# A Fourier transform over 3008 rows, split as 47 x 64 instead of 94 x 32, with both of its small-matrix stages in tiles of the TensorE array

## The chip, the cores and the metric

The kernel runs on one core of a Trainium2 chip. The metric is the device time of one execution in microseconds (us), as a median of several executions. A trace (one profiled execution) gives every instruction's start and length on each engine. PE is TensorE's matrix multiply and PEld its weight load, DVE is VectorE, ACT ScalarE, POOL GpSimd, SP the sync engine; a q after a name (DVEq, SPq) is that engine's sequencer, which issues its instructions and transfers; "L207" is line 207 of the kernel that is being shown.

## The reference

```python
def _attn_ref(x):                       # x: 8 batches x 3008 x 256, float32
    X = np.fft.fft(x, axis=1)           # over s, 3008 long
    X = np.fft.fft(X, axis=2)           # over d, 256 long
    return X.real.astype(np.float32)

def _moe_ref(x, w_in, w_out):           # x: 24064 x 256, w_in 256 x 2048, w_out 2048 x 256
    h = x @ w_in
    g = h * (1.0 / (1.0 + np.exp(-1.702 * h)))
    return (g @ w_out).astype(np.float32)
```

## The kernel before

The transform over d is folded into the first weight matrix once. The transform over s is done in two stages: s = 32 a + j, with a = 0..93 and j = 0..31. A first stage multiplies, for each j, by a matrix over a; a second stage multiplies by a small matrix over j. Between them the data changes its layout by a trip through memory. Both stages of the next batch are cut into pieces which are strung between the large products of the present one (`hidden`, which writes the banks pa and pb, and `product`, which writes po; 384 steps in all).

```python
NA, NB = 94, 32

def mix1(b, c):                                   # first stage, two values of j; 8 such groups a batch
    ...
    ps = bank("ps1")
    for i in range(2):
        jj, o = 2 * c + i, i * D
        if jj:
            nc.tensor.matmul(ps[0:96, o:o + D], lhsT=mat(w1, jj), rhs=t[:, NB - jj, :], start=True, stop=True)
            continue
        ...                                       # j = 0: four products of half the width
    nc.scalar.copy(full[:, 2 * c:2 * c + 2, :].rearrange("p j d -> p (j d)"), ps[0:96, :])

def stage2(b, blk, cs):                           # second stage, half a block; 3 blocks a batch
    ...
    ps = bank("ps2")
    for g in range(4):
        nc.tensor.matmul(ps[:, g * 128:(g + 1) * 128], lhsT=t4[:, 4 * blk + g, cs * H:(cs + 1) * H],
                         rhs=m2[:, cs, :], start=True, stop=True)
    nc.scalar.copy(pq[:, cs, :], ps[:])
```

The banks of PSUM come from a ring of four (`bank`), shared with the two banks of `hidden`. The first batch has its own code: VectorE folds four pieces, the products follow, and the layout changes by a direct move from SBUF to SBUF (`shuffle_first`).

## Time and profile before

| | before |
|---|---|
| time, median of 3 (lowest, highest) | 1971.92 us (1971.71, 1972.20) |
| span of the profiled execution | 1969.6 us |
| TensorE / VectorE / ScalarE busy | 98% / 79% / 35% |
| first large product starts at | 54.6 us |
| the two stages' share of the chain that ended last | 2.3% + 2.3% |

The way to read it: TensorE is busy without a gap from 330 to 1800 us, so it alone sets the end there; only its time is worth saving. The lines for this stand in the prediction.

### The profile page before, as it was taken

How to read it: one execution, taken by the hardware profiler on the slowest of the kernel's cores; microseconds unless marked ns; L12 is line 12 of the kernel's file. 1: busy time of each engine (PE TensorE's matmuls, PEld its weight loads, DVE VectorE, ACT ScalarE, POOL GpSimd, SP SyncE). 2: the span in 40 equal slices, each digit the busy share in tenths (PEclk: the TensorE clock that was granted, in tenths of full speed). 3: DMA queues.
4: the chain of work that ended last, by engine and by line, in shares of the span. 5: the costliest groups of instructions: out<-in, count | busy, mean ns of one | idle time of the engine just before them, and what ended most of it. 6: DMA issues, size and time to landing. Idle time of an engine off the chain costs nothing.

```text
span 1969.6 us, 26665 instructions
## 1 busy us (share of the span) xinstructions
PE 1938.4 (98%) x9290; PEld 1724.3 (88%) x9290; DVE 1555.3 (79%) x2893; ACT 695.8 (35%) x970; POOL 793.8 (40%) x1065
## 2 busy tenths in 40 slices
PE   6999999999999999999999999999999999999997
PEld 4698899988989889888899888998899988989886
DVE  4778788888788777887788878887878888778776
ACT  2633333333333333333333333333333333333332
POOL 5476323543245332463325622255323543223232
PEclk8999999999999999999999999999999999999999
DMA  6720441216202252123422252221611213202201
GB/s 197 204 46 11 82 85 15 46 43 121 17 11 48 52 111 17 16 51 57 98 20 45 37 98 42 24 47 43 113 22 14 17 44 58 17 11 23 21 11 22
DMA packets 241837, 101.31 MB, mean 51 GB/s; under 512 B 209651, under 2 KB 232561, under 8 KB 239713
## 3 DMA queue, kind: packets, MB, share of 16 engines
q1 hardware_dynamic: 238965, 97.42, 28.7%
q10 hardware_dynamic: 2736, 2.18, 0.4%
q8 instruction: 73, 1.20, 0.3%
q14 instruction: 63, 0.52, 0.1%
HBM read 56.28 MB, written 45.76 MB: 52 GB/s over the span
## 4 chain that ended last, share of the span: by engine, by line
PE 96%; ACT 1%; DMA 1%; DVE 1%; issue 0%; POOL 0%; DVEq 0%; SPq 0%; POOLq 0%
PE po L464 58%; PE pa L397 16%; PE pb L397 16%; PE ps L189 2%; PE ps L277 2%; DMA raw<-in_moe_w_in_dram 0%; DMA t<-xt 0%; PE ps L241 0%; PE psw L366 0%; PE ps L240 0%; ACT g L314 0%; ACT r L322 0%; ACT r L321 0%; PE psa L372 0%; PE ps L192 0%
## 5 line engine op out<-in xcount | busy, mean ns | idle before, releaser
L438 POOL TENSOR_TENSOR s<-h 128x256 f32<-128x256 f32 (+2 forms) x376 | 273.8, 728 | 1098.2 <-ACT h L426 1026.6
L464 PE MATMUL po<-s,wt 128*128 128x256 f32 (+2 forms) x2256 | 600.0, 375 | 0.0
L401 ACT COPY v<-pa 128x512 f32<-128x512 f32 (+2 forms) x384 | 221.6, 577 | 893.1 <-PE pa L397 893.1
L411 DVE TENSOR_TENSOR h<-v,pb 128x512 f32<-128x512 f32 (+2 forms) x384 | 259.3, 675 | 336.6 <-PE pb L397 329.1
L464 PEld LDWEIGHTS po<-s,wt 128*128 128x128 f32 x2256 | 428.8, 190 | 48.3
L464 PE MATMUL po<-h,wo 128*128 128x256 f32 (+2 forms) x1632 | 469.9, 375 | 0.0
L421 DVE TENSOR_TENSOR h<-v,dif 128x512 f32<-128x512 f32 (+3 forms) x512 | 436.1, 871 | 13.2
L426 ACT ACTIVATE h<-h 128x1024 f32<-128x1024 f32 (+2 forms) x384 | 400.8, 1044 | 11.1 <-DVE h L421 11.1
L397 PE MATMUL pa<-pq,wcs 128*128 128x256 f32 (+2 forms) x1536 | 389.0, 376 | 0.0
L397 PE MATMUL pb<-pq,wcs 128*128 128x256 f32 (+2 forms) x1536 | 387.7, 375 | 0.0
L464 PEld LDWEIGHTS po<-h,wo 128*128 128x128 f32 x1632 | 310.1, 190 | 35.4
L414 DVE SCALAR_TENSOR_TENSOR dif<-nb,af,pb 128x256 f32<-128x256 f32 (+2 forms) x768 | 328.3, 469 | 0.0
L397 PEld LDWEIGHTS pb<-pq,wcs 128*128 128x128 f32 x1536 | 291.9, 190 | 33.0
L397 PEld LDWEIGHTS pa<-pq,wcs 128*128 128x128 f32 x1536 | 287.3, 190 | 33.0 <-issue 0.8
L439 POOL TENSOR_TENSOR s<-h 128x256 f32<-128x256 f32 (+2 forms) x376 | 277.6, 738 | 0.0
L442 DVE TENSOR_TENSOR s<-h,s 128x256 f32<-128x256 f32 (+2 forms) x376 | 211.3, 562 | 13.0
L464 PE MATMUL po<-h,wt 128*128 128x256 f32 (+2 forms) x752 | 220.5, 375 | 0.0
L464 PE MATMUL po<-s,wo 128*128 128x256 f32 (+2 forms) x752 | 220.5, 375 | 0.0
L441 DVE TENSOR_TENSOR s<-s,h 128x256 f32<-128x256 f32 (+2 forms) x376 | 175.3, 466 | 1.2 <-POOL s L438 1.2
L464 PEld LDWEIGHTS po<-s,wo 128*128 128x128 f32 x752 | 142.9, 190 | 16.1
L464 PEld LDWEIGHTS po<-h,wt 128*128 128x128 f32 x752 | 142.9, 190 | 16.1
L195 ACT COPY xt<-ps 96x512 f32<-96x512 f32 x56 | 32.5, 581 | 161.0 <-PE ps L189 151.2
(76 smaller groups left out, 878.0 us busy)
## 6 DMA issues: line engine op xcount, KB each, us to landing
out_dram<-os SPq DMA_DIRECT2D x512, 32.0 KB
Td<-xt SPq DMA_DIRECT2D x7, 1536.0 KB
t<-Td SPq DMA_DIRECT2D x7, 1536.0 KB
Xr<-in_x_dram SPq DMA_DIRECT2D x7, 1410.0 KB
xt<-in_x_dram SPq DMA_DIRECT2D x7, 1280.0 KB
xt<-Xr SPq DMA_DIRECT2D x7, 1200.0 KB
out_dram<-os SPq DMA_DIRECT2D x248, 28.0 KB
nb<-pq SPq DMA_DIRECT2D x23, 256.0 KB
```

The lines of the kernel that those rows point to most:

```text
L189: nc.tensor.matmul(ps[0:96, o:o + D], lhsT=mat(w1, jj), rhs=t[:, NB - jj, :], start=True, stop=True)
L397: nc.tensor.matmul(ps[:, i * 256:i * 256 + n], lhsT=wcs[cs][:, f * 128:(f + 1) * 128], rhs=pq[:, cs, ks], start=True, stop=True)
L401: nc.scalar.copy(two(v[:], n), two(pa[:], n))
L411: nc.vector.tensor_tensor(two(h[:], n), two(v[:], n), two(pb[:], n), op=ALU.add)
L414: nc.vector.scalar_tensor_tensor(dif[:, i * 256:i * 256 + n], nb[:, ks], af2[:, f:f + 1], pb[:, i * 256:i * 256 + n], op0=ALU.mult, op1=AL ...
L421: nc.vector.tensor_tensor(free(h[:], 512 + at + m - 1, [256, 2], [NB, blocks], [-1, m]), *ins, op=ALU.add)
L426: nc.scalar.activation(g, g, ACTF.Gelu_apprx_sigmoid)
L438: eng.tensor_tensor(s1, a21, a22, op=ALU.add)
L439: eng.tensor_tensor(s3, a11, a21, op=ALU.subtract)
L441: eng.tensor_tensor(s2, s1, a11, op=ALU.subtract)
L442: eng.tensor_tensor(s4, a12, s2, op=ALU.subtract)
L464: nc.tensor.matmul(pot[q][:, i, :n], lhsT=lhs, rhs=rhs, start=(p == 0 and i == 0 and f == 0), stop=(p == NP - 1), skip_group_check=True)
```

## The change

Intent: neither stage fills the array. The first uses 94 rows and 96 columns, the second a block-diagonal matrix that is three quarters zeros. With s = 64 a + j, a = 0..46, each product fits a quarter of the array (47 of 64 rows, 48 of 64 columns), and four can run at once. In the second stage a product needs 64 rows and 32 columns, so eight fit. Since the small matrix is now the stationary operand, the result comes out turned, and VectorE turns it back in 32x32 blocks.

The core of the diff (loading, folding, the tables, the stores and the start's calls are cut):

```diff
-NA, NB = 94, 32
+NA, NB = 47, 64
...
-    def mix1(b, c):
+    def mix1(b, m):
...
+        ps = [bank("ps1") for _ in range(2)]
+        for i in (2 * m, 2 * m + 1):
+            for r in range(2):
+                for c in range(2):
+                    rows, o = slice(64 * r, 64 * r + NA), ps[r][64 * c:64 * c + 64, i % 2 * D:(i % 2 + 1) * D]
+                    jj = 16 * c + 8 * r + i
+                    if jj:
+                        nc.tensor.matmul(o, lhsT=mat(jj, rows), rhs=xt[rows, 31 - (8 * c + i), :], start=True, stop=True)
+                        continue
...
-    def stage2(b, blk, cs):
...
-        nc.scalar.copy(pq[:, cs, :], ps[:])
+    def stage2(b, blk):
+        pq, t4 = pqp.tile([128, 2, 512], F32, tag="pq", name="pq"), t4t[b]
+        pqt[b, blk] = pq
+        ps = [bank("ps2") for _ in range(NU)]
+        for cs in range(2):
+            for h in range(2):
+                for g in range(4):
+                    for u in range(NU):
+                        rows, at = slice(64 * u, 64 * u + 64), cs * 256 + h * 128
+                        nc.tensor.matmul(ps[u][32 * g:32 * g + 32, at:at + 128], lhsT=m2[rows, cs, h * RUN:(h + 1) * RUN],
+                                         rhs=t4[rows, 4 * blk:4 * blk + 4, cs * H + 32 * g:cs * H + 32 * g + 32],
+                                         start=True, stop=True)
+        for u in range(NU):
+            for cs in range(2):
+                nc.vector.transpose(free(pq[:], cs * 512 + u * RUN, [256, 2], [NU * RUN, 4], [1, RUN]),
+                                    free(ps[u][:], cs * 256, [128, 2], [32, 4], [1, 32]))
...
+    load_first(0, 4, nc.sync)
+    load_first(4, 4, nc.scalar)
+    load_first(8, 8, nc.sync)
...
-    for c in range(4):
-        fold_first(c)
-        if c:
-            mix_first(2 * c - 2)
-            mix_first(2 * c - 1)
...
-    shuffle_first(nc.scalar, 2, 3)
-    shuffle_first(nc.sync, 0, 1)
+    for r in range(2):
+        for m in range(4):
+            fold_first(r, m)
+            mix_first(r, m)
+        spill(0, 8 * r, 8 * r + 8, (nc.sync, nc.scalar))
+    fill(0, 0, 4)
```

## The prediction

> **What bounds the kernel now.** I read the page's busy shares first, then the chain that ended last by line, then busy time by stretch, and at last the groups and the order in time of the two stages that the change touches.
>
> The chain says who sets the end:
>
> ```profile
> PE 96%; ACT 1%; DMA 1%; DVE 1%; issue 0%; POOL 0%; DVEq 0%; SPq 0%; POOLq 0%
> by line: PE po L464 57.7%; PE pa L397 16.4%; PE pb L397 16.3%; PE ps L189 2.3%; PE ps L277 2.3%; DMA raw<-in_moe_w_in_dram 0.5%; DMA t<-xt 0.4%; issue 0.3%; PE ps L241 0.3%; PE psw L366 0.3%; PE ps L240 0.2%; ACT g L314 0.2%; ACT r L321 0.2
> ```
>
> The TensorE is 96% of the chain. L464, L397 are the two large products, which the change leaves alone; L189 is the first stage of the transform over s, L277 the second. Together the two stages are 4.6% of 1969.6 us, 91 us: that is all the change can reach, apart from the start.
>
> Busy time by stretch (start and end, length, then each engine's busy us):
>
> ```profile
> core 0: us, PE busy (x) PEld busy (x) DVE busy (x) ACT busy (x) POOL busy (x), PEclk, DMA share, GB/s
> 330.00:1800.00 1470.00, 1470.00 (x7123) 1319.62 (x7122) 1182.69 (x2237) 518.26 (x721) 592.51 (x821) 1.00 0.28 46
> 0.00:54.60 54.60, 38.63 (x128) 25.76 (x129) 22.29 (x26) 12.47 (x26) 29.88 (x25) 0.87 0.70 203
> ```
>
> From 330 to 1800 us the TensorE has no idle time at full clock, VectorE is busy 80%, ScalarE 35%, DMA 28%. So a nanosecond of TensorE saved there is one of the end, until VectorE is full; and a transfer or a ScalarE copy saved is worth nothing. The first 54.6 us are a start with its own limits.
>
> How long the touched work takes (start, length, count):
>
> ```profile
> 418.45 1.03 PE L189 MATMUL ps<-xt,w 94*96 94x256 f32 x4
> 419.31 1.03 PE L397 MATMUL pa<-pq,wcs 128*128 128x256 f32 x4
> ...
> 428.81 1.05 PE L277 MATMUL ps<-small,t 128*128 128x128 f32 x8
> 429.70 0.60 PE L397 MATMUL pa<-pq,wcs 128*128 128x256 f32 x2
> ```
>
> One fp32 product in the source is two MATMUL instructions (4 for the two products of a first-stage step). From first start to the next line's start, 4 instructions of 256 columns take 0.86 us (215 ns each), 8 of 128 columns 0.89 us (111 ns each). The modelled length of one (378 and 275 ns by the line views) exceeds that interval by 164 ns: the tail a successor hides, and a drain would expose.
>
> ```profile
> L277 PEld LDWEIGHTS ps<-small,t 128*128 128x128 f32 x384 | 51.9, 197 | 2.7
> L189 PEld LDWEIGHTS ps<-xt,w 94*96 94x96 f32 x210 | 33.8, 163 | 8.5
> ```
>
> Weight loads: 128 columns take a median of 192 ns, 96 columns 163: some 28 ns per 32 columns over a fixed part. At 111 ns an instruction, stage two sits at both limits at once, streaming 128 columns and loading 128 columns.
>
> **What the Trainium skill says.** "TensorEngine Tiling (Array Packing)", Key Properties: tiles work independently and can load weights and multiply in parallel, but changing the tiling mode drains the engine. "TensorE: Matmul & The Clock Gate", LDWEIGHTS: a load takes its columns / 1.2 ns, whatever the rows; the 28 ns per 32 columns above agree (27). Same page, Part 3 (The mechanism): matmuls of different tiles start about 4 ns apart, yet starts are strictly in program order. "VectorE: DVE Perf Modes", The three transpose paths: VectorE transposes within 32 by 32 blocks only, which is what the new layout of stage two is made for; the trace has 94 such instructions of 128x512, 687 ns each. No matmul in a column tile smaller than the array stands in this trace, so neither concurrency nor the drain can be checked.
>
> **The change, part by part.**
>
> *First stage, batches 1 to 7.* Before, per batch: 15 products of 256 columns = 30 instructions x 215 = 6.45 us, and for j = 0 four half-width products = 8 x 110 = 0.88 us: 7.3 us. After: four groups of 8 products (16 instructions) spread over four 64x64 tiles, so 4 per tile x 215 = 0.86 us; the first group has j = 0's eight half-width instructions in one tile, 0.88 + 0.43 = 1.31 us. Sum 3.9 us. Saved 3.4 x 7 = 24 us if four tiles really run at once. Loading 64 columns at 53 ns, 16 times one after the other, is 0.85 us as well, so serial loads would just fit.
>
> *Second stage, 24 blocks.* Before: 16 x 111 = 1.78 us a block. After: 32 products = 64 instructions of 128 columns over eight 64x32 tiles: 8 per tile x 111 = 0.89 us. Saved 0.89 x 24 = 21 us at best. But 64 weight loads of 32 columns are 64 x 27 = 1.73 us if they go one after another: then nothing is saved. I count on partly parallel loads (two row tiles): 14 us.
>
> *Drains, added.* 28 first-stage groups and 23 steady second-stage blocks stand between 128x128 work, at different steps. Going in exposes the 164 ns tail and a short load (28 to 55 ns and some fixed part), coming out the tail of a smaller tile and 107 ns of load: my estimate from those durations is 0.35 us per group and both ways. 51 x 0.35 = 18 us.
>
> *Evictions.* 48 ScalarE copies go (ScalarE is idle 65%: no gain); 96 VectorE transposes of 256 columns come, at about 0.41 us (half of 687 plus a fixed part, an estimate) = 39 us, VectorE 79% to 81%. A step of 4.7 us has some 1 us of VectorE slack; a block adds 1.6 us once in 16 steps, made up in the next. The two stages now take two banks of the ring of four at once. The next step's two banks are those of the current step, read until about 1.5 us after their products end, while product work of 3 us follows: no wait expected. I put 2 us on both.
>
> *Unchanged.* Columns per batch: 241 + 240 + 4x256 = 1505 before, 225 + 5x256 = 1505 after. GpSimd's folds: the same 16 pairs, more partitions, same length.
>
> *Start.* The table shrinks from 1.63 to 0.87 MB, matmuls use two column tiles, VectorE folds in 16 instructions of up to 508 columns (about 11 us against 15.1). Against that, the direct shuffle (8.7 us on the chain) becomes a spill to memory and a fill, two trips. Net estimate -3 us.
>
> Sum: -24 - 14 + 18 + 2 - 3 = -21 us: about 1950 us, -1.1%.
>
> **The rivals.**
> 1. *Tiles overlap only in pairs.* If starts are in order and a product's second instruction must wait for the first in its own tile, every product costs one interval: stage one 8 x 0.22 + 0.2 = 2.0 us a group against 1.72 (+8 us over all with j = 0), stage two 32 x 0.11 + 0.1 = 3.7 against 1.78 us (+45 us), drains +18: about 2040 us. For it: the two instructions per product, one after the other, at one tile; the skill's strict order. Against: nothing in this trace; the order of the loops, which changes tile with each product, was chosen for concurrency.
> 2. *Weight loads bind serially.* Stage two saves nothing: -24 + 18 - 1 = -7: 1965 us. For it: 111 ns is already the load limit in stage two.
> 3. *Drains are nearly free, all loads parallel.* -24 - 21 + 5 - 3 = -43: 1929 us. For it: short instructions have short tails.
> 4. *VectorE becomes the bound* round the blocks: 24 x up to 1 us = +24 us, 1974. Against: 20% idle, three steps of lag in the schedule.
>
> **Range and chances.** The sum lies between rivals 2 and 3, which a range of 1926 to 2010 holds together; rival 1 is the long tail above (1 in 6 or so). Faster by over 2% (below 1932.5) needs rival 3 in full and some of the start: 0.2. Slower by over 2% (above 2011.4) needs rival 1: 0.17. Within: 0.63.
>
> **What would show each step.** In the changed trace: the time from the first matmul of a first-stage group to the next large product (0.86 + 0.35 right, 2.0 or more says rival 1); the same for a second-stage block (0.9 to 1.3 right, 1.7 rival 2, 3.7 rival 1); the gap between the last large product before a group and its first matmul, and after it (the drains); TensorE idle before the large products for a bank held by a transpose (rival 4); the start of the first pa product against 54.6 us. The prediction is wrong if the steady stretch loses TensorE time to anything else, or if spill and fill at the start take longer than the 8.7 us they replace by over 5 us.

## The result, and the profile after

The changed kernel takes 1953.93 us (median of 4, 1952.88 to 1954.08) against 1972.06 us of the kernel before in the same rounds. The ratio is 0.9903, with a 95% interval of 0.9886 to 0.9920. (Ratios here are the mean time of one kernel's fast runs over that of the other's of the same rounds, so not quite the ratio of the medians quoted.) So the change is 1% faster, which lies within the 2% called the same; 1950 had been predicted.

The chain that ended last, by engine and by line:

```profile
PE 96%; ACT 1%; DVE 0%; DVEq 0%; issue 0%
by line: PE po L496 58.2%; PE pa L429 17.2%; PE pb L429 16.6%; PE ps L207 1.4%; PE ps L304 1.3%; PE psw L398 0.4%; PE ps L211 0.3%; PE psa L404 0.2%; ACT wcs L399 0.1%; ACT r L354 0.1%; ACT r L353 0.1%; ACT g L346 0.1%; PE psn L321 0.1%; AC
```

L207 is now the first stage and L304 the second: 2.7% of 1952.1 us in place of 4.6% of 1969.6, some 38 us less. The span fell by 17.5 us only, so part of it must be paid elsewhere: in this view the waits of a mode change go to the large products around it (pa grew from 16.4% to 17.2%).

Busy time by stretch, as for the kernel before:

```profile
330.00:1800.00 1470.00, 1470.00 (x8340) 1301.71 (x8339) 1219.03 (x2305) 501.38 (x694) 611.03 (x826) 1.00 0.32 46
0.00:54.60 54.60, 34.35 (x106) 15.16 (x106) 31.98 (x24) 10.49 (x22) 32.87 (x21) 0.72 0.66 166
```

In the steady stretch TensorE still has no idle time, and VectorE is at 83%. The first 54.6 us do less on TensorE than before (34.35 us against 38.63), at a lower mean clock (0.72 against 0.87), and move less data.

A second-stage block and a first-stage group, in order of time (start, length, what, count):

```profile
353.85 0.59 PE L496 MATMUL po<-h,wt 128*128 128x256 f32 x2
354.37 1.16 PE L304 MATMUL ps<-t,small 64*32 64x128 f32 x64
355.46 1.03 PE L429 MATMUL pa<-pq,wcs 128*128 128x225 f32 x4
356.32 0.92 PE L429 MATMUL pb<-pq,wcs 128*128 128x225 f32 x4
...
382.70 0.54 PE L496 MATMUL po<-s,wo 128*128 128x225 f32 x2
383.17 1.09 PE L207 MATMUL ps<-xt,w 47*64 47x256 f32 x16
384.20 1.03 PE L429 MATMUL pa<-pq,wcs 128*128 128x225 f32 x4
385.06 0.92 PE L429 MATMUL pb<-pq,wcs 128*128 128x225 f32 x4
```

The 64 instructions of a block take 1.09 us from start to the next line's start. The line before them lasts 0.52 us instead of the 0.43 that two 256-column instructions take elsewhere, and the pa products after them 0.86 instead of 0.76 (the interval of the pb line, also four of 225 columns: it starts at 356.32 and its successor at 357.08): 1.09 + 0.09 + 0.10 = 1.28 us for a block that cost 1.78 (two halves of 0.89). The group of 16 takes 1.03 + 0.09 + 0.10 = 1.22 us; two groups of the kernel before, which did the same work, took 2 x 0.86 = 1.72. The group with j = 0 takes 1.51 + 0.19 = 1.70 us against 2.16.

So a batch with all of its pieces should gain 3 x 0.50 + 3 x 0.50 + 0.46 = 3.46 us. I read the start of each step's first pa product from both traces and took the difference (after minus before):

```
step      before us    after us    after - before
0             54.60       63.91      +9.31
8            103.50      115.00     +11.50
48           303.70      311.75      +8.05
96           540.03      544.58      +4.54
144          776.37      777.40      +1.03
192         1012.70     1010.23      -2.47
288         1485.37     1475.88      -9.48
383         1944.19     1929.90     -14.29
end         1969.55     1952.09     -17.46
```

From batch to batch (48 steps) the gain is 3.50 us, as worked out from the pieces. But the changed kernel enters step 8 **11.5 us late**, and it gains 3.2 us after the last step's start. The account: +11.5 at the start, -25.8 in the steps, -3.2 at the end.

The end is plain from the order in time after the last transposes. Before:

```profile
1958.34 1.30 DVE L495 STREAM_TRANSPOSE os<-c 128x512 f32<-128x512 f32 x2
1959.07 7.47 SPq L512 DMA_DIRECT2D out_dram<-os  x16
1959.08 7.82 ACTq L512 DMA_DIRECT2D out_dram<-os  x16
```

After:

```profile
1944.94 1.30 DVE L527 STREAM_TRANSPOSE os<-c 128x512 f32<-128x512 f32 x2
1945.67 3.83 SPq L544 DMA_DIRECT2D out_dram<-os  x8
1945.68 3.94 ACTq L544 DMA_DIRECT2D out_dram<-os  x8
```

The last block has 256 columns now, not 240, so its stores come in whole pieces, half as many, and issuing them takes half the time.

The start, after (ScalarE's first work, then the loop of the first batch):

```profile
12.14 2.31 ACTq L233 DMA_DIRECT2D xt<-in_x_dram  x2
14.48 1.28 ACT L346 ACT_TABLE_LOAD   x1 [14.48 <-DMA xt<-in_x_dram]
15.78 1.12 ACT L346 ACTIVATE g<-raw 128x1024 f32<-128x1024 f32 x1
...
30.12 0.21 ACT L246 COPY e<-xt 128x8 f32<-128x8 f32 x1
30.43 1.98 PE L259 MATMUL ps<-e,w 128*64 128x256 f32 x8 [0.96 <-ACT e L246]
32.58 0.59 ACT L262 COPY xt<-ps 128x512 f32<-128x512 f32 x1 [2.24 <-DVE e L250]
33.06 0.21 ACT L246 COPY e<-xt 128x8 f32<-128x8 f32 x1
33.37 1.98 PE L259 MATMUL ps<-e,w 128*64 128x256 f32 x8 [0.96 <-ACT e L246]
```

In the kernel before, the square of the first weights (its `g<-raw`) started at 10.21 us. Here ScalarE is still issuing loads until 14.5, then squares at 15.78. VectorE rounds those weights before its first fold, which starts at 20.1 us against 16.2. Then comes the loop, 2.93 us a group: products, ScalarE's copy out of PSUM (L262), only then ScalarE's copy of the next group's edge columns (L246), for which the next products wait. From the last products to the first product of the transformed data the two kernels need the same: the last copy ends at 48.6 and the first product on the moved data (the small one ahead of stage two) comes at 57.8 us (9.2 us) against 39.0 and 48.8 (9.8 us). The spill through memory costs no more than the direct move did.

The clock differs too. From 18 to 50 us, before and after (the last figure but two is the granted clock):

```profile
18.00:50.00 32.00, 21.99 (x88) 17.38 (x89) 15.27 (x19) 7.97 (x17) 14.14 (x10) 0.83 0.56 155
18.00:50.00 32.00, 18.63 (x70) 8.27 (x71) 22.85 (x19) 5.65 (x16) 20.68 (x12) 0.52 0.56 141
```

From 50 to 75 us it is 0.95 before and 0.73 after. The eight instructions of a group take 1.98 us in the loop above, at half clock, and 1.08 us in a group of start_all (below) at full clock, so up to 0.9 us of each 2.93 us goes with the clock (an estimate from these two lengths). And 2.2 of the 11.5 us arise only between step 0 and step 8 of the table. No run held the clock fixed.

**Theory**, then: (1) in the steps the gain is TensorE's time in tiles, less a mode change of some 0.4 us for each group; (2) VectorE's extra work costs nothing; (3) the start lost 9 to 11 us to two orders on ScalarE, the loads ahead of the square and the copy out ahead of the next fold (with the clock's answer to them); (4) the end gained 3 us by fewer issues. **Rivals**: stage two's gain comes from ScalarE's copies that went, not from the tiles; VectorE bounds the steps around a block; the start is bound by data or by the trip through memory; or by the lower clock as such, for which there is no run. A further question, left by the prediction, is in which order the tiles start.

### The profile page after: what moved, and what is told of

Read it like the earlier page. It is cut to its first block, busy times and chain, and to the rows that moved or that the text cites. A ratio compares the mean times of both kernels' runs of the same rounds, so it can differ in the third digit from the quotient of the medians.

```text
span 1952.1 us, 29356 instructions
## 1 busy us (share of the span) xinstructions
PE 1916.0 (98%) x10664; PEld 1672.3 (86%) x10664; DVE 1586.4 (81%) x2925; ACT 665.0 (34%) x921; POOL 816.1 (42%) x1057
## 4 chain that ended last, share of the span: by engine, by line
PE 96%; ACT 1%; DVE 0%; DVEq 0%; issue 0%
PE po L496 58%; PE pa L429 17%; PE pb L429 17%; PE ps L207 1%; PE ps L304 1%; PE psw L398 0%; PE ps L211 0%; PE psa L404 0%; ACT wcs L399 0%; ACT r L354 0%; ACT r L353 0%; ACT g L346 0%; PE psn L321 0%; ACT h L458 0%; ACT L458 0%; PE psr L291 0%
## 5 line engine op out<-in xcount | busy, mean ns | idle before, releaser
L470 POOL TENSOR_TENSOR s<-h 128x256 f32<-128x256 f32 (+1 forms) x376 | 269.5, 717 | 1060.5 <-ACT h L458 996.3
L496 PE MATMUL po<-s,wt 128*128 128x256 f32 (+1 forms) x2256 | 599.7, 375 | 0.0
L433 ACT COPY v<-pa 128x512 f32<-128x512 f32 (+1 forms) x384 | 221.8, 577 | 1065.0 <-PE pa L429 1064.9
L443 DVE TENSOR_TENSOR h<-v,pb 128x512 f32<-128x512 f32 (+1 forms) x384 | 258.7, 674 | 260.0 <-PE pb L429 252.5
L496 PE MATMUL po<-h,wo 128*128 128x256 f32 (+1 forms) x1632 | 469.6, 375 | 0.0
L453 DVE TENSOR_TENSOR h<-v,dif 128x512 f32<-128x512 f32 (+1 forms) x448 | 413.4, 934 | 13.2
L458 ACT ACTIVATE h<-h 128x1024 f32<-128x1024 f32 (+1 forms) x384 | 400.7, 1043 | 19.6 <-DVE h L453 19.5
L429 PE MATMUL pa<-pq,wcs 128*128 128x256 f32 (+1 forms) x1536 | 395.8, 380 | 0.0
L429 PE MATMUL pb<-pq,wcs 128*128 128x256 f32 (+1 forms) x1536 | 388.8, 376 | 0.0
L429 PEld LDWEIGHTS pa<-pq,wcs 128*128 128x128 f32 x1536 | 287.8, 191 | 47.8 <-issue 14.5
L446 DVE SCALAR_TENSOR_TENSOR dif<-nb,af,pb 128x256 f32<-128x256 f32 (+1 forms) x768 | 328.0, 468 | 0.5 <-DMA nb<-pq 0.5
L471 POOL TENSOR_TENSOR s<-h 128x256 f32<-128x256 f32 (+1 forms) x376 | 287.0, 763 | 0.0
```

Of the source, the lines that this page charges most:

```text
L429: nc.tensor.matmul(ps[:, i * 256:i * 256 + n], lhsT=wcs[cs][:, f * 128:(f + 1) * 128], rhs=pq[:, cs, ks], start=True, stop=True)
L433: nc.scalar.copy(two(v[:], n), two(pa[:], n))
L443: nc.vector.tensor_tensor(two(h[:], n), two(v[:], n), two(pb[:], n), op=ALU.add)
L446: nc.vector.scalar_tensor_tensor(dif[:, i * 256:i * 256 + n], nb[:, ks], af2[:, f:f + 1], pb[:, i * 256:i * 256 + n], op0=ALU.mult, op1=AL ...
L453: nc.vector.tensor_tensor(free(h[:], 512 + at + m - 1, [256, 2], [RUN, blocks], [-1, m]), *ins, op=ALU.add)
L458: nc.scalar.activation(g, g, ACTF.Gelu_apprx_sigmoid)
```

## The experiments

Eleven kernels, all derived from the changed one; all gave the right result. "Span" is that of the profiled execution; the changed kernel's is 1952.1 us.

### s2_plain: stage two back on the whole array

```diff
-        ps = [bank("ps2") for _ in range(NU)]
-        for cs in range(2):
-            for h in range(2): ...                     # 32 products in 64x32 tiles, 4 transposes by VectorE
+        for cs in range(2):
+            ps = bank("ps2")
+            for g in range(4):
+                nc.tensor.matmul(ps[:, g * 128:(g + 1) * 128], lhsT=t4[:, 4 * blk + g, cs * H:(cs + 1) * H],
+                                 rhs=m2[:, cs, :], start=True, stop=True)     # m2 block-diagonal again
+            nc.scalar.copy(free(pq[:], cs * 512, [RUN, 8], [256, 2], [1, RUN]),
+                           free(ps[:], 0, [64, 8], [32, 2], [1, RUN]))
```

> The changed kernel with its second stage put back on the whole array (eight products of 128x128 weights and 128 columns in a block, copied out by ScalarE), the first stage left in tiles. Theory (each tiled group of stage two saves 0.5 us of TensorE: 0.9 us of streaming less, 0.4 us of mode change more): 23 steady blocks x 0.51 = 12 us slower than the changed kernel, 1965 to 1967 us, and in its trace again 0.89 us per eight instructions with no gap around a block. Rival (the gain of stage two comes from ScalarE's copies or VectorE's transposes, or stage two gains nothing because loads bind): within 3 us of the changed kernel's 1954.

Measured: 1963.53 us (1961.52 to 1965.36), ratio to the kernel before 0.9954. Step starts differ from the changed kernel's by 0.50 us a block, 11.4 us at step 383, and the span is 11.5 us longer. A block in its trace (L301 is stage two there):

```profile
355.23 0.59 PE L489 MATMUL po<-h,wt 128*128 128x256 f32 x2
355.66 1.95 PE L301 MATMUL ps<-small,t 128*128 128x128 f32 x16
357.44 0.93 PE L422 MATMUL pa<-pq,wcs 128*128 128x225 f32 x4
358.21 0.92 PE L422 MATMUL pb<-pq,wcs 128*128 128x225 f32 x4
```

The neighbours have their undisturbed intervals again (0.43 and 0.77 us), and the block takes 1.78. Stage two's tiles are worth 11.5 us net; the first stage keeps the rest. The median lies below the 1965 to 1967 us expected. The executions of this kernel lie further apart than the others' (four in two pairs, 1961.6 us with a mean granted clock of 0.990 and 1965.35 us with 0.987), so the median alone would give the 11.5 only within some 2 us; the trace is of the second pair, whose clock is that of the changed kernel's trace, and its step starts (0.13 us apart at step 8) give it directly.

### s2_products_twice: what a product costs without the mode change

```diff
-                for g in range(4):
+                for g in (0, 1, 2, 3, 0, 1, 2, 3):
```

> Every product of a second-stage block is done twice, same result, nothing else touched: the marginal cost of a block's products without its mode change. Theory (eight tiles stream at once, 109 ns a round, the mode change is a fixed 0.4 us): a block goes from 1.28 to 2.15 us, 24 x 0.87 = 21 us slower than the changed kernel, about 1975 us. Rival a (the instructions' supply or weight loads bind at the 17 ns per product seen late in a block): more, up to 0.55 us... no more than 1 us a block, so not told from theory by time alone but by rounds of 8 instructions over 109 ns in the trace. Rival b (most of a block's 1.28 us is fixed): under 10 us.

Measured: 1980.79 us (1978.75 to 1982.17), ratio 1.0044; the span is 26.7 us longer than the changed kernel's. Each block from step 56 on adds 0.87 us:

```profile
363.55 2.03 PE L304 MATMUL ps<-t,small 64*32 64x128 f32 x128
365.51 1.03 PE L429 MATMUL pa<-pq,wcs 128*128 128x225 f32 x4
```

128 instructions take 1.96 us against 1.09 for 64. So 64 more cost 0.87 us, which is eight rounds of 0.109 with eight tiles at once: neither weight loads nor the supply of instructions bind. The fixed part of a block is 1.28 - 0.87 = **0.41 us, the price of going into tiles and back**. The total came out 6 us above the expectation. 3.1 of it arises at the second batch's first block (step 40), where the last three of the 128 instructions start 2.7 us after the others and the profile names no engine that they waited for; the rest lies in the start (3.5 us at step 8). The wait at step 40 I did not follow further.

### s1_same_tile and s2_same_tile: the order of the tiles

```diff
 # s1_same_tile                                   # s2_same_tile
-        for i in (2 * m, 2 * m + 1):              -        for cs in range(2):
-            for r in range(2):                    -            for h in range(2):
-                for c in range(2):                -                for g in range(4):
+        for r in range(2):                        -                    for u in range(NU):
+            for c in range(2):                    +        for g in range(4):
+                for i in (2 * m, 2 * m + 1):      +            for u in range(NU):
                                                   +                for cs in range(2):
                                                   +                    for h in range(2):
```

> First stage with the loop over i innermost: the two products of one tile follow each other directly (four instructions to one tile in a row) instead of going round the four tiles. Theory (each tile takes its own instructions from the queue, so order between tiles does not matter[...]): no change, 1953 to 1955 us, and groups of 1.03 us. Rival (matmuls start strictly in program order[...]): a group takes about 13 intervals of 0.216 = 2.8 us, 28 x 1.7 = 48 us slower, about 2002 us.

> Second stage with the loops over the two halves innermost: eight instructions in a row for one tile, then the next tile. Theory (own order per tile, but [...]at first only four tiles have work): a block takes 0.2 to 0.5 us longer, 5 to 12 us over all, 1959 to 1966 us. Rival (strict program order): 8 tiles x 7 x 0.109 = 6.2 us a block, over 110 us slower, 2070 us.

Measured: s1_same_tile 1955.94 us (ratio 0.9919), span 2.1 us longer than the changed kernel's; s2_same_tile 2028.76 us (ratio 1.0287), span 76 us longer. The starts of the 16 instructions of a first-stage group in s1_same_tile, as the trace has them (four a line):

```
383.772 383.785 383.799 383.812
384.039 384.052 384.065 384.079
384.255 384.268 384.281 384.295
384.470 384.484 384.497 384.510
```

The program has the four instructions of a tile one after the other, and yet four start together, then four more 0.216 us later. The trace names no tile, but each round shows that an instruction occupies its tile for 0.216 us, so four starts within 0.04 us belong to four tiles. Strict program order is refuted: each tile takes up its own instructions. The groups grew by only 0.02 us (1.05 for 1.03), the one with j = 0 by 0.23 us. There one tile has ten instructions in a row.

In stage two the same freedom breaks down:

```profile
366.76 0.59 PE L496 MATMUL po<-h,wt 128*128 128x256 f32 x2
367.29 4.32 PE L304 MATMUL ps<-t,small 64*32 64x128 f32 x64
371.54 1.03 PE L429 MATMUL pa<-pq,wcs 128*128 128x225 f32 x4
```

A block takes 4.25 us, which neither theory nor rival had (1.3 to 1.6 and 7.3). The starts, read as one series for each tile, show why: the first tile's eight instructions start at 367.285, .419, .528, .637, .746, .855, .965 and 368.074; the second tile's first at 367.752, just after the first tile's **fifth**. The third begins 0.467 us after the second, and so on. New theory: a tile can hold about four matmuls and their loads waiting; when a fifth in a row for it comes, everything behind it waits. These eight instructions (four matmuls, four loads) are an eighth of 64, and 64 is an estimate of what is taken up ahead: in the trace of s2_two_in_row (below) the clean rounds end after 32 matmuls with their 32 loads. With four tiles the share would be 16, or eight matmuls: the ten in a row of the j = 0 group exceed it by two, 2 x 0.11 = 0.22 us, and 0.23 was measured. That second figure was known when the share was worked out, and no run tests the share for four tiles.

### s2_two_in_row: is it a share of four?

```diff
-            for h in range(2):
-                for g in range(4):
-                    for u in range(NU):
+            for g in range(4):
+                for u in range(NU):
+                    for h in range(2):
```

> Second stage with only the loop over the halves innermost: two products, so four instructions, in a row for one tile, then the next tile. Theory formed on s2_same_tile (there a new tile began when the tile before had started its fifth of eight instructions: with eight tiles each has room for about four matmuls with their loads, an eighth of the queue): four in a row fit, a block stays at 1.09 us within 0.15, total within 3 us of the changed kernel's 1954. Rival (instructions are handed out in program order, and any run for one tile holds up the others until its last has started): 16 visits x 3 x 0.109 = 5.2 us a block, or in a milder form, half of the 3.2 us that s2_same_tile added: over 30 us slower.

Measured: 1961.46 us (1960.31 to 1961.67), ratio 0.9947; the span is 6.4 us longer, a block takes 1.40 us, 0.32 more than the changed kernel's. That is outside both expectations, far nearer to the theory's. In the trace the first 32 instructions, four in a row for each of the eight tiles, start in four clean rounds of eight 0.109 us apart. The delay lies in the second half of the block, where instructions now arrive 0.033 us a tile: two products at the 17 ns a product at which, in the changed kernel too, instructions come once the first 64 are used up. So four in a row do not hold up other tiles, as the share of four says. But in an order that serves the tiles one after the other, the rate of supply shows. That last part is read from one trace and was not tested by itself.

### dve_twice: VectorE's transposes done twice

```diff
-            for cs in range(2):
+            for cs in (0, 1, 0, 1):
                 nc.vector.transpose(...)
```

> Every transpose of VectorE out of a second-stage block is done twice, same result: 96 more instructions of 0.41 us, 39 us more of VectorE. Theory (VectorE has slack, nothing on TensorE waits for it): within 2 us of the changed kernel's 1954. Rival (VectorE bounds the steps around a block): 10 us or more slower, and TensorE idle in the steps after a block.

Measured: 1954.25 us (1953.54 to 1956.35), ratio 0.9906; from step 8 to the end the step starts stay 0.35 us *ahead* of the changed kernel's, without any drift. 96 more transposes at 0.41 us, some 39 us of VectorE work, cost nothing. VectorE is not the bound.

### start_sync, start_ahead, start_ahead_vector: the start

```diff
 # start_sync
-    load_first(4, 4, nc.scalar)
+    load_first(4, 4, nc.sync)
 # start_ahead
-    for r in range(2):
-        for m in range(4):
-            fold_first(r, m)
-            mix_first(r, m)
-        spill(0, 8 * r, 8 * r + 8, (nc.sync, nc.scalar))
+    groups = [(r, m) for r in range(2) for m in range(4)]
+    fold_first(*groups[0])
+    for g, (r, m) in enumerate(groups):
+        if g + 1 < len(groups):
+            fold_first(*groups[g + 1])
+        mix_first(r, m)
+        if m == 3:
+            spill(0, 8 * r, 8 * r + 8, (nc.sync, nc.scalar))
 # start_ahead_vector: start_ahead, and
-        for p, eng in ((slice(0, 64), nc.vector), (slice(64, 128), nc.gpsimd)):
+        for p, eng in ((slice(0, 64), nc.vector), (slice(64, 128), nc.vector)):
```

> The second quarter of the first batch's loads is issued from the sync engine's queue instead of ScalarE's. Theory (the start lost 4 us because ScalarE, held by issuing loads until 14.5 us, squared the first weights 5.6 us later than before, and VectorE's first fold followed it): first fold at 16 to 17 us instead of 20.1, end 2 to 4 us earlier, 1950 to 1952. Rival (the start is bound by data or by the spill and fill through memory): no change within 1 us.

> The fold of the next group is issued before the products of the present one, so ScalarE's copy of the next group's edge columns no longer stands behind its copy out of PSUM. Theory (the groups of the first batch run 2.93 us apart because each waits through ScalarE for the one before): the second half's groups come 2.0 us apart or less, end 3 to 6 us earlier, 1948 to 1951. Rival (VectorE's folds, slowed by GpSimd's beside them, set the pace): under 1.5 us.

> As start_ahead, and VectorE does the subtractions that GpSimd did (0.67 us each; with GpSimd beside it VectorE's fold instructions took 1.57 us). Theory (both hold the start): 5 to 9 us earlier than the changed kernel, 1945 to 1949. Rival (memory traffic sets the start): as start_ahead.

| kernel | median us | ratio | span less than the changed kernel's | first pa product at |
|---|---|---|---|---|
| start_sync | 1948.62 | 0.9877 | 5.1 us | 58.7 us |
| start_ahead | 1949.03 | 0.9878 | 4.7 us | 59.2 us |
| start_ahead_vector | 1948.02 | 0.9874 | 6.1 us | 57.3 us |

Putting either order on ScalarE right gives about 5 us by itself (start_sync more than the 2 to 4 expected), and from step 8 on every one of the three runs step for step like the changed kernel, within 0.1 us. The clock's share is in these figures: in start_ahead its mean from 18 to 50 us was 0.69, not 0.52. In start_sync the square starts at 8.80 us and the first fold at 15.0:

```profile
8.80 1.17 ACT L346 ACTIVATE g<-raw 128x1024 f32<-128x1024 f32 x1 [6.30 <-DMA raw<-in_moe_w_in_dram]
13.34 0.21 ACT L246 COPY e<-xt 128x8 f32<-128x8 f32 x1 [3.37 <-DMA xt<-in_x_dram]
```

Moving the subtractions to VectorE adds 1.4 us (1.0 by the medians) to what start_ahead saves: beside GpSimd's subtractions VectorE's folds had taken 1.57 us each, alone 0.69.

### tail_split: the last stores in two pieces each

```diff
+                if last:
+                    put(0, RUN, 7)
+                    put(7, RUN, 1)
+                    continue
                 put(0, RUN, whole)
```

> The last block's 16 stores are each split in two (7 places and 1), as the kernel before had them, so 32 issues instead of 16 on the two queues. Theory (3.5 us of the gain come from the end: the kernel before issues for 7.5 and 7.8 us after its last transpose, the changed one for 3.8 and 3.9): 3.3 to 4 us slower than the changed kernel, 1957 to 1958 us. Rival (the end is set by the last bytes' landing): under 1 us.

Measured: 1957.20 us (1956.32 to 1957.32), ratio 0.9924; the span is 3.3 us longer, and the last step starts where it did (0.18 us earlier). So the end alone gives 3.45 us back:

```profile
1945.49 7.49 SPq L544 DMA_DIRECT2D out_dram<-os  x16
1945.49 7.66 ACTq L544 DMA_DIRECT2D out_dram<-os  x16
```

### start_all: the three changes of the start together

The edits of start_sync and start_ahead_vector in one kernel.

> All three changes of the start together: loads off ScalarE's queue, the fold one group ahead, VectorE doing both subtractions. Theory (the first half of the start was held by ScalarE's late squares, 5 us, the second by the folds; the data of the second half land at 27.4 us, as start_sync shows, then four groups of about 2.05 us follow): the first pa product at 54 to 55 us instead of 63.9, end 8 to 10 us earlier than the changed kernel, 1944 to 1946 us, ratio to the kernel before 0.986. Rival (the parts remove the same wait, whichever is done): no more than the best part alone, 1948 us.

Measured: **1945.41 us** (1945.01 to 1945.86), ratio 0.9865 with a 95% interval of 0.9850 to 0.9880; the span is 8.7 us shorter than the changed kernel's. It beats both kernels. The first pa product is at 55.38 us (54 to 55 expected). The parts give 5.1 and 6.1 us alone and 8.7 together, so they overlap. The first batch's second half is what remains (start, length, count, idle before):

```profile
21.21 5.81 PE L259 MATMUL ps<-e,w 128*64 128x256 f32 x24 [0.83 <-ACT e L246]
28.81 1.08 PE L259 MATMUL ps<-e,w 128*64 128x256 f32 x8 [1.79 <-DVE e L250]
31.69 1.97 PE L259 MATMUL ps<-e,w 128*64 128x256 f32 x8 [1.79 <-DVE e L250]
```

The products now wait for VectorE's folds of the second half, which in start_sync could not begin before its data landed at 27.4 us (here they begin at 26.7, also after a wait for data). The same eight instructions take 1.08 us at full clock (28.81) and 1.97 at half (31.69).

## Why the prediction was right or wrong

The total was right (1950 predicted, 1953.9 measured), in part by luck, because errors cancelled: the steps gained 7.8 us more than the 18 of the sum, the start came out 14.5 us worse, and the end gave 3.2 that no term had. By its steps:

- **First stage, "24 us if four tiles really run at once".** Right. The four tiles start 0.006 us apart and take four rounds of 0.216 us. With the mode change taken apart, a group streams for 0.86 us, as worked out.
- **Second stage, "I count on partly parallel loads (two row tiles): 14 us".** This term was mis-sized. The loads bind nothing: eight rounds of 0.109 us are 0.87 us a block, with 64 loads in it, 14 ns for each and not 27. 1.78 - 0.87 = 0.91 us a block over 23 steady blocks is 21 us, the "best" of the prediction.
- **Drains, "0.35 us per group and both ways. 51 x 0.35 = 18 us".** Right within its rounding: 0.41 us in stage two (s2_products_twice), 1.22 - 0.86 = 0.36 in stage one; 23 x 0.41 + 28 x 0.36 = 19.5 us. The estimate came from the trace of before alone: the 164 ns that an instruction lasts beyond its interval, and the time of an exposed weight load.
- **Evictions, "I put 2 us on both".** Nothing (dve_twice). The 0.41 us for a transpose of 256 columns was exact.
- **Start, "Net estimate -3 us".** This step failed: it was +11.5 us at step 8. What was wrong was not the part that I feared. The spill and fill took no longer than the direct move. I counted the work of each engine and did not follow the order on ScalarE's queue: loads issued there ahead of the square (5.1 us, start_sync), and each group's copy out of PSUM standing in front of the next group's fold (4.7 us, start_ahead). Both were to be read in the diff. One size was wrong as well: VectorE's 16 folds took 21.9 us and not 11, most of them 1.57 us each beside GpSimd's. And no term allowed for the clock (0.52 in place of 0.83 from 18 to 50 us). In a change worth some 20 us, a start of 54.6 us with its own limits deserved that reading.
- **The end.** Not foreseen: half the issues on both queues, -3.4 us (tail_split).

The sum as measured: -24 - 21 + 19.5 = -25.5 us in the steps (the step starts say -25.8), +11.5, and -3.2 at the end: -17.5 us (-17.2 with the -25.5). Three slips of the prediction change nothing: 192 - 163 is 29 ns, rival 1's block is 3.6 us, and its table sizes mix units (1632 KB against 848 KB).

Of the rivals, the first (tiles overlap only in pairs) and the second (weight loads bind) are refuted by the rounds of eight and four in the traces; the fourth (VectorE) by dve_twice; the third was half right, the loads are parallel but the drains are not free.

What stays open: how much of the start's loss is the clock's; the 2.7 us that start_all is still behind the kernel before at step 8 (106.2 us against 103.5; only 0.8 of it stands at step 0, and from 50 to 75 us the clock was 0.78 against 0.95), the cause of the one wait of 3.1 us in s2_products_twice, and whether the rate of supply explains the whole 0.32 us of s2_two_in_row.

## What to carry to other kernels

Where TensorE is the bound, small products in tiles gain what the rounds say, less a fixed 0.4 us for each change of mode, so gather many of them between two changes; go round the tiles in the loop order, because a run of products for one tile soon holds up the rest. And when a change touches a prologue, read the order of the instructions on each engine's queue, not only the sum of its work: here two orders on an engine that is 65% idle, with subtractions shared between two engines, cost 8.7 us of a gain of 25.8 us in the steps, and putting them right gave the fastest version.

## What the Trainium skill lacked or had wrong

- "TensorE: Matmul & The Clock Gate", Part 3 (What overlaps and what doesn't), states that matmuls start and end strictly in program order. That does not hold between tiles: in s1_same_tile, with four instructions in a row for each of four tiles, four started within 0.04 us and the next four from 0.27 us after the first; in strict order the second of these would have had to wait for its own tile.
- "Advanced Engine Details and Errata", Engine Queue Depths, says of TensorE's 64 only that it is complicated with tiling. The runs fit a queue that is shared out among the tiles: with eight tiles a new one began when the tile before had started its fifth of eight instructions (block of 4.25 us instead of 1.09), with four tiles ten in a row cost 0.23 us.
- "TensorEngine Tiling (Array Packing)", Key Properties, says that a change of mode drains the engine and gives no size: 0.41 us in and out for 64x32 tiles with 128 columns, 0.36 us for 64x64 with 256, between fp32 products on the whole array.
- No page that I read gives the rate at which fp32 products in tiles run: eight 64x32 tiles did eight instructions of 128 columns in 0.109 us and four 64x64 tiles four of 256 in 0.216 us, each the interval of one such instruction on the whole array.
